# Sinkhorn normalisation with rows on the partitions, column sums on the matrix engine, in a fused attention and feed-forward kernel

## The chip, the cores and the metric

The kernel runs on one core of a Trainium2 chip. A core has a matrix engine (TensorE, PE in the profile; PEld is its weight load), a vector engine (VectorE, DVE), a scalar engine (ScalarE, ACT), GpSimdE (POOL) and SyncE (SP), which only starts transfers here. They work side by side and wait for each other on semaphores. Sixteen DMA engines move data between HBM and the core's memory. Matrix products land in PSUM, which has eight banks (p0 to p7 in this kernel).

The metric is the device time of one execution in microseconds (us); lower is better. The time before is a median of 3 runs. One execution was also profiled; its span runs from its first to its last instruction.

## The reference

Four batches of eight heads each have 768 tokens of 64 features, cut into eight blocks of 96. A small matrix per head, 8x8, is normalised five times by rows and columns (Sinkhorn). With it the blocks of K and V are mixed; then each block of Q attends to the mixed block at its place, and a gated feed-forward layer follows.

```python
P = sort_net                                   # [4, 8, 8, 8]
for _ in range(5):
    P = P - np.max(P, axis=-1, keepdims=True)
    P = np.exp(P)
    P = P / (np.sum(P, axis=-1, keepdims=True) + 1e-09)
    P = P / (np.sum(P, axis=-2, keepdims=True) + 1e-09)
k_sorted = np.einsum('bhij,bhjcd->bhicd', P, k_b).reshape(B, H, S, D)
v_sorted = np.einsum('bhij,bhjcd->bhicd', P, v_b).reshape(B, H, S, D)
...
scores = scale * np.matmul(q_b, k_sb.transpose(0, 1, 2, 4, 3))
attn = softmax(scores)
x = np.matmul(attn, v_sb)                      # to [3072, 512]
...
g = x @ w_gate
out = (g * sigmoid(g) * (x @ w_val)) @ w_out
```

## The kernel before

Work goes in eight units of 384 tokens, two per batch. For each unit the kernel forms scores, softmax, attention output (`xt`) and then the feed-forward products: `g` and `u` (line 520, 12 chunks of 128 features), and the down product (line 548). All matrix work is BF16. The order of all steps is written out by hand in the string `ORDER`; a loop at the end of the kernel calls the step of each word with its arguments, and every engine runs its instructions strictly in that order. A word names the step, its indices, the engine that copies the result out of PSUM (`a` ACT, `d` DVE) and the PSUM bank.

Ahead of `ORDER` stands the opening, which the change is about:

- Loads. SP loads the 32 small matrices (`p_sb`, one per partition, 64 values). POOL issues all large loads, in this order: first half of q of batch 0, K and V of batch 0, weights, the other half of q, and so on. POOL also makes the identity `ident` between the issues.
- Sinkhorn, lines 322 to 338. All 32 matrices lie on 32 partitions, with 64 values each. ACT takes the exponential (331); DVE makes the row sums (332), their reciprocals (333) and products (334), the column sums through a transposed view (335), reciprocals (336) and products (337). The maximum is subtracted once, ahead of the first exponential. Five iterations follow each other, each step dependent on the one before.
- Fills. `busy` (line 245) runs matrix products on constants that nobody reads, so that PE is not idle: 64 of 112 columns at first, and 8 of 112, 10 of 512 and 4 more during the last iterations. `ORDER` has more of them at waits in the first unit.
- `q0_piece` (lines 249 to 259) turns the first q heads, 12 transposes on PE and one ACT copy each, in the fourth and the fifth iteration.
- `make_zk` and `make_bdk` (372 to 388) bring the result to the place where the block mix wants it: `selk` copies each matrix's row of 64 values to the partitions (h, j, ch) of its head on PE, DVE multiplies with a mask and sums (`zk`, `zkr`), and a product with another mask gives `bdk`, a block-diagonal 128x128 matrix per batch. Batch 0 is made on DVE before `ORDER`; the step `late` makes the other three, on POOL.
- Block mix. `k_piece` and `v0_piece` call `mix` (line 283), 16 products per piece of `bdk` with the raw K or V. `ORDER` begins with `late`, five K pieces (`kp`), three V pieces (`v0f`), the sixth K piece, and the scores of the first unit (`tqk`, line 404). K and V are mixed only after their load has landed and `bdk` is there.

Of the kernel before, what the change touches and what calls it, by code (L numbers as in the profile page):

```python
# [9 lines left out]
FP32 = mybir.dt.float32  # L10
BF16 = mybir.dt.bfloat16
# [10 lines left out]
tmt,0,0,a v0f,1,d,p2 v0f,0,a,p3 tst,0,0 texp,0,0 ldv,2 texp,0,2 ldwo,0 v0f,4,d,p6 busy,3,p2 v0t,0,0,d,p7  # L22
v0t,1,0,d,p2 v0t,0,1,a,p3 tav,0,0,p0,p1 tdiv,0,0 v0t,1,1,a,p6 tav,0,1,p4,p5 tdiv,0,1 busy,2,p2 txt,0,0,d,p7
tav,0,2,p2,p3 tdiv,0,2 tav,0,3,p0,p1 txt,0,1,d,p6 q0p,1,0,a,p4 q0p,1,1,a,p5 txt,0,2,a,p7 g,0,2,p2,0,2 g,0,1,p3,0,2
tdiv,0,3 txt,0,3,a,p6 tqk,1,0,p0,p1 tmax,1,0 tqk,1,1,p4,p5 tmax,1,1 vp,1,5,a,p7 g,0,2,p2,2,3 g,0,1,p3,2,3
u,0,1,p6,0,2 ldwo,1 g,0,2,p2,3,4 th,0,2 gs,0,2 g,0,0,p7,0,2 u,0,1,p6,2,3 ldq,3 tmt,1,0,a g,0,1,p3,3,4 th,0,1
u,0,1,p6,3,4 tmt,1,1,d gs,0,1 g,0,0,p7,2,3 tst,1,0 texp,1,0 tst,1,1 texp,1,1 g,0,0,p7,3,4 th,0,0 gs,0,0 us,0,1
hp,0,1 u,0,0,p2,0,2 ldk,2 u,0,2,p3,0,2 u,0,0,p2,2,3 vp,1,3,a,p0 u,0,2,p3,2,3 vp,1,4,d,p1 u,0,2,p3,3,4 h,0,2
u,0,0,p2,3,4 vp,1,2,d,p4 us,0,0 hp,0,0 g,0,3,p5 th,0,3 gs,0,3 u,0,3,p6 h,0,3 kp,1,0,a,p7 kp,1,1,a,p0 g,0,4,p2
th,0,4 gs,0,4 u,0,4,p1 us,0,4 hp,0,4 tqk,1,3,p3,p4 tmax,1,3 tqk,1,2,p5,p6 tmax,1,2 kp,1,2,d,p7 kp,1,3,a,p0  # L30
kp,1,5,a,p2 g,0,5,p1 th,0,5 gs,0,5 u,0,5,p0 us,0,5 hp,0,5 tmt,1,2,a tmt,1,3,d g,0,6,p2 th,0,6 gs,0,6 u,0,6,p7 h,0,6
tst,1,3 texp,1,3 tst,1,2 texp,1,2 tav,1,0,p0,p1 tdiv,1,0 g,0,7,p2 th,0,7 gs,0,7 u,0,7,p7 us,0,7 hp,0,7 txt,1,0,d,p3
tav,1,1,p4,p5 tdiv,1,1 g,0,8,p6 th,0,8 gs,0,8 u,0,8,p0 us,0,8 hp,0,8 tav,1,2,p1,p2 tdiv,1,2 g,0,9,p7 th,0,9 gs,0,9
u,0,9,p3 us,0,9 hp,0,9 txt,1,1,a,p4 vp,1,1,a,p5 txt,1,2,a,p6 g,0,10,p0 th,0,10 gs,0,10 u,0,10,p1 us,0,10 hp,0,10
vp,1,0,a,p2 vtrip,1 ldk,3 g,1,0,p7,0,3 tav,1,3,p3,p4 tdiv,1,3 g,0,11,p5 th,0,11 gs,0,11 u,0,11,p6 us,0,11 hp,0,11
u,1,0,p1,0,3 txt,1,3,d,p0 kp,1,4,d,p2 qp,1,2,d,p3 qp,1,1,d,p4 qp,1,0,d,p5 g,1,0,p7,3,4 th,1,0 gs,1,0 u,1,0,p1,3,4
us,1,0 hp,1,0 g,1,1,p6 th,1,1 gs,1,1 u,1,1,p0 us,1,1 hp,1,1 qk,2,1,p2,p3 rmax,2,1 shift,2,1 expo,2,1 qk,2,2,p4,p5
rmax,2,2 shift,2,2 qp,1,3,a,p1 rsum,2,1 norm,2,1 expo,2,2 rsum,2,2 g,1,2,p7 th,1,2 gs,1,2 u,1,2,p6 us,1,2 hp,1,2
dn,0,2,0,3,p0 dn,0,1,0,4,p2 dn,0,2,3,6 g,1,3,p3 th,1,3 gs,1,3 u,1,3,p1 h,1,3 dn,0,1,4,8 norm,2,2 g,1,4,p4 th,1,4
gs,1,4 dn,0,2,6,9 u,1,4,p5 us,1,4 hp,1,4 ldv,3 g,1,5,p6 th,1,5 gs,1,5 u,1,5,p7 us,1,5 hp,1,5 qk,2,0,p3,p4 rmax,2,0  # L40
# [69 lines left out]
def kernel(  # L110
# [34 lines left out]
    C0 = UT // 128  # L145

# [71 lines left out]
    p_sb = const.tile([BH, NB + 1, NB], FP32, name="p_sb")  # L218
    nc.sync.dma_start(out=p_sb[:, 0:NB, :], in_=sort_net.rearrange("b h i j -> (b h) i j"))
    load_q0(0)  # L220
    load_k(0)
# [5 lines left out]

    fill = const.tile([128, 512], BF16, name="fill")
# [13 lines left out]
    def busy(n, b, cols=512):  # L242

        for _ in range(n):
            nc.tensor.matmul(ps(b, [cols]), lhsT=fill[:, 0:128], rhs=fill[:, 0:cols], start=True, stop=True)  # L245
# [76 lines left out]
    nc.vector.memset(p_sb[:, NB:NB + 1, :], 1e-9)  # L322
    P = p_sb[:, 0:NB, :]
    pbf = const.tile([BH, NB, NB], BF16, name="pbf")
    rowred = const.tile([BH, NB, 1], FP32, name="rowred")
    colred = const.tile([BH, 1, NB], FP32, name="colred")
    nc.vector.reduce_max(rowred[:, :, 0], P, axis=AX.X)
    nc.vector.tensor_tensor(P, P, rowred.to_broadcast([BH, NB, NB]), op=ALU.subtract)
    busy(64, "p7", 112)
    for it in range(N_ITER):  # L330
        nc.scalar.activation(P, P, AF.Exp)
        nc.vector.reduce_sum(rowred[:, :, 0], P, axis=AX.X)
        nc.vector.reciprocal(rowred, rowred)
        nc.vector.tensor_mul(P, P, rowred.to_broadcast([BH, NB, NB]))
        nc.vector.reduce_sum(colred[:, 0, :], p_sb.transpose([0, 2, 1]), axis=AX.X)
        nc.vector.reciprocal(colred, colred)
        nc.vector.tensor_mul(pbf if it == N_ITER - 1 else P, P,
                             colred.to_broadcast([BH, NB, NB]))
        if it == N_ITER - 2:
            q0_piece(0, 0, "a", "p0")  # L340
        if it == N_ITER - 1:
            q0_piece(0, 1, "a", "p1")
            busy(8, "p7", 112)
            busy(10, "p7")
            for _ in range(4):
                nc.tensor.matmul(ps("p7", [UT]), lhsT=fill[:, 0:128], rhs=tr["q", 0][:, HP - 1].rearrange("p i c -> p (i c)"),
                                 start=True, stop=True)
# [42 lines left out]
    def late(b):  # L390
        make_zk(1, B, b)
        for n in range(1, B):
            make_bdk(n, nc.gpsimd)
# [222 lines left out]
```

## Time and profile before

| what | value |
|---|---|
| median of 3 runs | 265.04 us (264.96 to 265.06) |
| the profiled execution, its own time | 265.16 us |
| its span | 263.1 us |
| PE busy | 254.7 us, 97% |
| DVE, ACT, POOL busy | 190.3, 154.2, 116.8 us |
| SP: landing of the small matrices, first DVE step on them | 2.34 us |
| `bdk` of batch 0 done on DVE | 12.75 us |
| first product of the K mix | 13.00 us |
| first product of the V mix | 15.08 us |
| first scores | 17.14 us |

The times in the lower half are counted from the start of the span. In a line of the timeline stand start, length, engine, line of the kernel, operation, what is written and read with its shape, how many instructions are merged, and in brackets how long the engine was idle before and what ended that idle time. A matmul's shape is given as the outputs and columns, such as `128x512`. In the DMA views, packets are counted by size; a share of "16 engines" is the part of all engines' time that the packets of a queue took.

### The profile page before, as it was taken

To read this page: it belongs to the slowest core of one execution; us is meant where nothing else is said; L and a number is where in the kernel's file an instruction comes from. 1 tells how busy PE (TensorE), PEld (TensorE's weight loads), DVE (VectorE), ACT (ScalarE), POOL (GpSimd) and SP (SyncE) were. 2 spreads that over 40 slices of the span, in tenths; PEclk is the share of its full clock that TensorE was granted. 3 is DMA by queue.
4 is the path that set the end of the run, shared out by engine and by line. 5 is a ranking of instruction groups with operands and counts; after the bars stand their busy time and mean duration, and the time that the engine had idled before them with its cause. 6 is when DMAs were issued, how large, how long until landed. Compare 5 with 4: busy or idle time off the path is not lost.

```text
span 263.1 us, 6835 instructions
## 1 busy us (share of the span) xinstructions
PE 254.7 (97%) x2766; PEld 157.1 (60%) x2766; DVE 190.3 (72%) x345; ACT 154.2 (59%) x299; POOL 116.8 (44%) x152
## 2 busy tenths in 40 slices
PE   7878999999999999999999999999999999999995
PEld 7456766665566555665566555665566555655553
DVE  5775877689688896779798776977897778632460
ACT  3246787755467467866476767586566665544422
POOL 8732342433856437135632475226544672431220
PEclk9999999999999999999999999999999999999999
DMA  6999999999980902100294005920110021002103
GB/s 82 215 199 209 216 203 211 204 238 248 157 195 0 161 2 82 44 0 2 120 118 123 2 0 199 118 49 1 52 70 0 2 80 42 0 1 83 40 0 120
DMA packets 33695, 25.60 MB, mean 97 GB/s; under 512 B 21376, under 2 KB 29312, under 8 KB 33664
## 3 DMA queue, kind: packets, MB, share of 16 engines
q0 software_dynamic: 11104, 14.16, 31.4%
q1 hardware_dynamic: 22560, 11.02, 18.2%
q8 instruction: 21, 0.34, 0.5%
q14 instruction: 10, 0.08, 0.1%
HBM read 30.68 MB, written 8.65 MB: 149 GB/s over the span
## 4 chain that ended last, share of the span: by engine, by line
PE 88%; DMA 5%; DVE 3%; issue 1%; ACT 1%; POOL 1%; DVEq 0%; POOLq 0%
PE ps_ps L520 47%; PE ps_ps L548 23%; DMA vn<-in_v_dram 5%; PE ps_ps L497 3%; PE ps_ps L404 3%; PE ps_ps L283 3%; PE ps_ps L508 2%; PE ps_ps L309 2%; PE ps_ps L433 1%; PE ps_ps L270 1%; PE ps_ps L560 1%; DVE qt L240 1%; DVE xn L455 1%; PE ps_ps L447 1%; DVE v L240 0%
## 5 line engine op out<-in xcount | busy, mean ns | idle before, releaser
L539 POOL TENSOR_TENSOR h<-u_sb,gs 128x384 bf16<-128x384 f32 x65 | 58.6, 911 | 64.9 <-DVE gs L533 36.3
L520 PE MATMUL ps_ps<-xt,wg_sb 128*128 128x384 bf16 x384 | 79.8, 327 | 0.0
L520 PE MATMUL ps_ps<-xt,wv_sb 128*128 128x384 bf16 x384 | 79.6, 326 | 0.0
L533 DVE SCALAR_TENSOR_TENSOR gs<-th,ps_ps 128x384 bf16<-128x384 bf16 x96 | 51.4, 543 | 32.4 <-ACT th L525 32.0
L548 PE MATMUL ps_ps<-wo_sb,h 128*128 128x512 bf16 x276 | 70.5, 380 | 0.0
L525 ACT ACTIVATE th<-ps_ps 128x384 bf16<-128x384 f32 x96 | 46.9, 490 | 34.2 <-PE ps_ps L520 32.1
L490 POOL TENSOR_TENSOR en<-e,rs 96x384 bf16<-96x384 f32 x48 | 38.5, 822 | 55.6 <-DVE rs L485 31.1
L520 PEld LDWEIGHTS <-wv_sb 128*128 128x128 bf16 x384 | 37.2, 98 | 24.8
L520 PEld LDWEIGHTS <-wg_sb 128*128 128x128 bf16 x384 | 35.5, 98 | 25.9
L548 PEld LDWEIGHTS <-h 128*128 128x128 bf16 x276 | 26.3, 98 | 25.3 <-issue 0.2
L529 ACT ACTIVATE u_sb<-ps_ps 128x384 f32<-128x384 f32 x65 | 31.8, 490 | 10.9 <-PE ps_ps L520 7.6
L480 ACT ACTIVATE e<-e 96x768 f32<-96x768 f32 x24 | 20.2, 841 | 23.8 <-DVE e L477 23.8
L484 DVE TENSOR_REDUCE rs<-e 96x8 f32<-96x768 f32 x24 | 22.6, 941 | 10.3 <-ACT e L480 10.3
L473 DVE TENSOR_REDUCE rm<-ps_ps 96x8 f32<-96x768 f32 x24 | 22.8, 949 | 4.8 <-PE ps_ps L404 4.3
L477 DVE TENSOR_TENSOR e<-ps_ps,rm 96x768 f32<-96x768 f32 x24 | 22.9, 953 | 0.8
L541 DVE SCALAR_TENSOR_TENSOR h<-ps_ps,gs 128x384 bf16<-128x384 f32 x31 | 17.2, 557 | 2.7
L238 ACT COPY o_sb<-ps_ps 128x512 f32<-128x512 f32 x16 | 9.2, 580 | 8.6 <-PE ps_ps L548 8.6
L497 PEld LDWEIGHTS <-en 96*96 96x96 bf16 x192 | 12.0, 125 | 3.2
L245 PE MATMUL ps_ps<-fill 128*128 128x112 bf16 (+1 forms) x96 | 11.7, 290 | 2.2 <-DVE p_sb L322 1.5
L497 PE MATMUL ps_ps<-ident,en 96*96 96x96 bf16 x192 | 12.5, 209 | 0.0
L238 ACT COPY et<-ps_ps 96x768 bf16<-96x768 bf16 x13 | 10.3, 791 | 3.2 <-PE ps_ps L497 3.1
L238 ACT CAST kt<-ps_ps 128x512 bf16<-128x512 f32 x14 | 7.8, 593 | 3.8 <-PE ps_ps L283 3.7
(97 smaller groups left out, 240.6 us busy)
## 6 DMA issues: line engine op xcount, KB each, us to landing
out_dram<-o_sb SPq DMA_DIRECT2D x23, 256.0 KB, 2.0
kn<-in_k_dram POOLq DMA_DIRECT2D x4, 768.0 KB, 18.6
vn<-in_v_dram POOLq DMA_DIRECT2D x4, 768.0 KB, 14.4
qn<-in_q_dram POOLq DMA_DIRECT2D x3, 768.0 KB, 23.6
vscr<-vm SPq DMA_DIRECT2D x3, 768.0 KB, 3.3
vt<-vscr SPq DMA_DIRECT2D x3, 768.0 KB, 7.9
wg_sb<-in_moe_w_gate_dram POOLq DMA_DIRECT2D x3, 512.0 KB, 18.7
wv_sb<-in_moe_w_val_dram POOLq DMA_DIRECT2D x3, 512.0 KB, 20.4
```

The lines of the kernel that those rows point to most:

```text
L238: nc.scalar.copy(dst, src)
L473: nc.vector.reduce_max(m[:, :, :, 0], st["s", u, hp], axis=AX.X)
L477: nc.vector.tensor_tensor(e, st["s", u, hp], st["m", u, hp].to_broadcast([BLK, 2, HB, BLK]), op=ALU.subtract)
L484: nc.vector.reduce_sum(rs[:, :, :, 0], st["e", u, hp], axis=AX.X)
L490: nc.gpsimd.tensor_tensor(en[:, x], st["e", u, hp][:, x], st["rs", u, hp][:, x].to_broadcast([BLK, HB, BLK]), op=ALU.mult)
L497: nc.tensor.transpose(p[:, x * HB + i, :], st["en", u, hp][:, x, i, :], ident[0:BLK, 0:BLK])
L520: nc.tensor.matmul(st[kind, u, m], lhsT=w[:, kc, ts(m, 128)], rhs=xt[u][:, kc, :], start=(kc == 0), stop=(kc == HP - 1))
L525: nc.scalar.activation(st["th", u, m], st["g", u, m], AF.Tanh, scale=0.5)
L529: nc.scalar.activation(st["us", u, m], st["u", u, m], AF.Copy, scale=0.5)
L533: nc.vector.scalar_tensor_tensor(gs, st["th", u, m], 1.0, st["g", u, m], op0=ALU.add, op1=ALU.mult)
L539: nc.gpsimd.tensor_tensor(h_t[u][:, m, :], st["us", u, m], st["gs", u, m], op=ALU.mult)
L548: nc.tensor.matmul(st["o", u, t], lhsT=h_t[u][:, m, ts(t, 128)], rhs=wo_sb[:, m, :], start=(m == 0), stop=(m == NFC - 1))
```

## The change

The Sinkhorn part is written anew, with what it needs before and after:

- The 256 rows of the 32 matrices lie on the 128 partitions, in two groups `g` of two batches each, with 8 values per row. SP loads them so.
- `exp` on ACT gives the row sums in the same step (`accum_out`), the first one with the maximum as bias. DVE takes the reciprocal and multiplies (`R`, with 1e-9/8 added for the column sum's epsilon).
- The column sums are an FP32 matrix product on PE: `same` is a 128x128 matrix of ones where two rows belong to one head, made from `blk`, which POOL fills with a memset and two selects between the loads of q and K. DVE takes the reciprocal straight from PSUM and multiplies `E`, the row reciprocal and the column reciprocal in one step. The two groups take turns step by step.
- In the last iteration the values are spread by a mask over the heads (`XE`, `X`), and `spread`, one product with `rowi`, puts them where the block mix wants them. `bdk` of batch 0 is made by DVE straight from PSUM; `late` copies the rest once (`z`) and makes three products on POOL as before. `selk`, `mjk`, `pbf`, `zk` and `zkr` are gone.
- A one-element exponential (`warm`) stands at the start of ACT's work.
- The fills are other ones: 48 of 64 columns that write a quarter of the outputs each in turn, 27 of 80 columns, 2 and 13 of 80 in the first iteration, three of 512 in each of the next three, none after. Two groups of fills are gone from `ORDER` (three after `v0f,4`, two after `tdiv,0,1`), and four before the K mix.
- Both q pieces are in the last iteration.

```diff
-    p_sb = const.tile([BH, NB + 1, NB], FP32, name="p_sb")
-    nc.sync.dma_start(out=p_sb[:, 0:NB, :], in_=sort_net.rearrange("b h i j -> (b h) i j"))
+    P = const.tile([128, G, NB], FP32, name="p_sb")
+    nc.sync.dma_start(out=P, in_=sort_net.rearrange("(g b) h i j -> (b h i) g j", b=2))
     load_q0(0)
+    blk = const.tile([128, 2 * H], FP32, name="blk")
+    nc.gpsimd.memset(blk, 1.0)
+    nc.gpsimd.affine_select(out=blk, in_=blk, pattern=[[-NB, 2 * H]], base=0, channel_multiplier=1,
+                            compare_op=ALU.is_ge, fill=0.0)
+    nc.gpsimd.affine_select(out=blk, in_=blk, pattern=[[NB, 2 * H]], base=NB - 1, channel_multiplier=-1,
+                            compare_op=ALU.is_ge, fill=0.0)
     load_k(0)
     load_v(0)
...
+    warm = const.tile([128, 1], FP32, name="warm")
+    nc.vector.memset(warm, 0.0)
+    nc.scalar.activation(warm, warm, AF.Exp)
...
+        for i in range(n):
+            if quarters:
+                r = ts(i % 4, 32)
+                nc.tensor.matmul(ps(b, [cols])[r], lhsT=fill[:, 0:32], rhs=fill[:, 0:cols], start=True, stop=True)
+                continue
             nc.tensor.matmul(ps(b, [cols]), lhsT=fill[:, 0:128], rhs=fill[:, 0:cols], start=True, stop=True)
...
-    nc.vector.reduce_max(rowred[:, :, 0], P, axis=AX.X)
-    nc.vector.tensor_tensor(P, P, rowred.to_broadcast([BH, NB, NB]), op=ALU.subtract)
-    busy(64, "p7", 112)
+    nc.vector.tensor_reduce(nmax, P, axis=AX.X, op=ALU.max, negate=True)
+    same = const.tile([128, 2 * H, NB], FP32, name="same")
+    nc.vector.tensor_copy(same, blk.unsqueeze(2).to_broadcast([128, 2 * H, NB]))
...
+    fills = [((2, "p7", 80), (13, "p7", 80)),
+             ((0, "p7", 80), (3, "p7", 512)),
+             ((0, "p7", 80), (3, "p7", 512)),
+             ((0, "p7", 80), (3, "p7", 512))]
+    busy(48, "p7", 64, True)
+    busy(27, "p7", 80)
     for it in range(N_ITER):
-        nc.scalar.activation(P, P, AF.Exp)
-        nc.vector.reduce_sum(rowred[:, :, 0], P, axis=AX.X)
-        nc.vector.reciprocal(rowred, rowred)
-        nc.vector.tensor_mul(P, P, rowred.to_broadcast([BH, NB, NB]))
-        nc.vector.reduce_sum(colred[:, 0, :], p_sb.transpose([0, 2, 1]), axis=AX.X)
-        nc.vector.reciprocal(colred, colred)
-        nc.vector.tensor_mul(pbf if it == N_ITER - 1 else P, P,
-                             colred.to_broadcast([BH, NB, NB]))
...
-            busy(8, "p7", 112)
-            busy(10, "p7")
...
+        last = it == N_ITER - 1
+        for g in range(G):
+            nc.scalar.activation(E[g], P[:, g, :], AF.Exp, bias=nmax[:, g:g + 1] if it == 0 else 0.0,
+                                 accum_out=rs[g])
+        for g in range(G):
+            nc.vector.reciprocal(rs[g], rs[g])
+            nc.vector.tensor_scalar(R[g] if last else R[g][:, :, 0], wide(E[g]) if last else E[g], rs[g], 1e-9 / NB,
+                                    op0=ALU.mult, op1=ALU.add)
+        if last:
             q0_piece(0, 0, "a", "p0")
+        for g in range(G):
+            nc.tensor.matmul(colsum[g][:, 0:NB * CH if last else NB], lhsT=same.rearrange("p c i -> p (c i)"),
+                             rhs=R[g].rearrange("p j ch -> p (j ch)") if last else R[g][:, :, 0], start=True, stop=True)
+            if not last:
+                busy(*fills[it][g])
+            elif g == 1:
+                q0_piece(0, 1, "a", "p1")
+        for g in range(G):
+            if last:
+                nc.vector.tensor_tensor(XE[g].rearrange("p h (j ch) -> p h j ch", ch=CH),
+                                        mask8.unsqueeze(2).unsqueeze(3).to_broadcast([128, H, NB, CH]),
+                                        E[g].unsqueeze(1).unsqueeze(3).to_broadcast([128, H, NB, CH]), op=ALU.mult)
+                nc.vector.reciprocal(cs[g], colsum[g])
+                nc.vector.scalar_tensor_tensor(X[g], XE[g], rs[g], cs[g].unsqueeze(1).to_broadcast([128, H, NB * CH]),
+                                               op0=ALU.mult, op1=ALU.mult)
+            else:
+                nc.vector.reciprocal(cs[g][:, 0:NB], colsum[g][:, 0:NB])
+                nc.vector.scalar_tensor_tensor(P[:, g, :], E[g], rs[g], cs[g][:, 0:NB], op0=ALU.mult, op1=ALU.mult)
...
-            nc.gpsimd.tensor_copy(selk, ident[0:BH, 0:BH].unsqueeze(2).to_broadcast([BH, BH, 16]))
+            mask8 = const.tile([128, H], FP32, name="mask8")
+            nc.vector.tensor_tensor(mask8, blk[:, 0:H], blk[:, H:2 * H], op=ALU.add)
...
-    def make_zk(b0, b1, b):
...
+    def spread(out, g):
+        nc.tensor.matmul(out.rearrange("p b i -> p (b i)"), lhsT=X[g].rearrange("p h c -> p (h c)"),
+                         rhs=rowi.rearrange("p b i -> p (b i)"), start=True, stop=True)
...
+    def late(bk):
+        p = ps(bk, [B, NB])
+        for g in range(G):
+            spread(p[:, ts(g, G), :], g)
+        z = const.tile([128, B - 1, NB], FP32, name="z")
+        nc.vector.tensor_copy(z, p[:, 1:B, :])
         for n in range(1, B):
-            make_bdk(n, nc.gpsimd)
+            make_bdk(n, nc.gpsimd, z[:, n - 1, :])
...
-    make_zk(0, 1, "p2")
-    make_bdk(0, nc.vector)
-    busy(4, "p7")
+    z0 = ps("p2", [G, NB])
+    spread(z0, 0)
+    make_bdk(0, nc.vector, z0[:, 0, :])
+    busy(0, "p7")
```

## The prediction

> **What bounds the kernel now.** I read the page first, then the waits of TensorE (PE) by stretches, then the chain that ended last up to 18 us, then the timeline of the first 18 us, and last the DMA view in narrow windows. On the page PE is busy for 254.7 of 263.1 us, so most of the span cannot be moved by this change. The waits of PE from 30 us on are one line:
>
> ```profile
> PE ps_ps L404 <- DVE qt L240: 0.3, 1, 0.3
> ```
>
> After 30 us PE runs one fixed order with 0.3 us of waiting. Whatever the start gains or loses goes through to the end one to one, and all that the change touches lies before. The chain in order of time says what sets the start (start, length, what):
>
> ```profile
> 2.86 12.18 DMA vn<-in_v_dram
> 15.04 0.04 issue
> 15.08 0.97 PE ps_ps L283 x48
> 16.05 1.09 ACT vT L238 x2
> ```
>
> The block mix of V waits until V has landed at 15.04. The Sinkhorn chain is not in it. The timeline shows how near it comes; one iteration, then its end:
>
> ```profile
> 6.37 0.26 ACT L331 ACTIVATE p_sb<-p_sb 32x64 f32<-32x64 f32 x1 [1.52 <-DVE p_sb L337]
> 6.66 0.21 DVE L332 TENSOR_REDUCE rowred<-p_sb 32x8 f32<-32x64 f32 x1
> 6.90 0.19 DVE L333 RECIPROCAL rowred<-rowred 32x8 f32<-32x8 f32 x1
> 7.13 0.21 DVE L334 TENSOR_TENSOR p_sb<-p_sb,rowred 32x64 f32<-32x64 f32 x1
> ...
> 7.91 0.21 DVE L337 TENSOR_TENSOR p_sb<-p_sb,colred 32x64 f32<-32x64 f32 x1
> ...
> 8.15 0.26 ACT L331 ACTIVATE p_sb<-p_sb 32x64 f32<-32x64 f32 x1 [1.52 <-DVE p_sb L337]
> ...
> 12.46 0.29 DVE L384 TENSOR_TENSOR bdk<-m,zkr 128x128 bf16<-128x128 f32 x1
> ...
> 13.00 1.46 PE L283 MATMUL ps_ps<-bdk,kn 128*64 128x64 bf16 x80
> ...
> 15.08 0.95 PE L283 MATMUL ps_ps<-bdk,vn 128*64 128x64 bf16 x48 [0.63 <-DMA vn<-in_v_dram]
> 15.86 0.42 PE L283 MATMUL ps_ps<-bdk,kn 128*64 128x64 bf16 x16
> ```
>
> An iteration takes 1.78 us (6.37 to 8.15). Dependent steps start 0.23 to 0.29 us apart, however small. The five K pieces run from 13.00 to 14.46, then PE waits 0.63 us for V. So the K pieces may start as late as 15.08 - 1.46 = 13.62 without moving anything; an earlier start gains nothing while V lands at 15.04.
>
> **The change part by part.**
>
> Loads. SP's first load brings 256 rows of 32 bytes in place of 32 rows of 256; it landed at 2.3. The nearest row for small pieces is the first q load: 942 packets below 512 B (the DMA window below) in some 2.4 us, 59 per engine, so 41 ns each; with 16 pieces per engine instead of 2 it lands 0 to 0.6 us later, and I take 0.3. POOL's queue gets a memset and two selects between the q load and the K load. Rows: a 128x1 memset 0.10, the select that makes ident 0.29, so K, V and all behind them are issued about 0.7 us later, until the removed selk copy (0.64) gives it back at the second V load. Cover: the queue moves data in order, and K's large packets follow q's small ones:
>
> ```profile
> DMA packets 1016, 0.81 MB, mean 203 GB/s; under 512 B 942, under 2 KB 942, under 8 KB 1016
> ```
>
> That is 4 to 8 us: q's small packets first, and the 74 large ones from 5.9 on, where the rate of the slices jumps. q's issue ran from 1.24 to 2.31 and its first packets went at 3.2, 0.9 us later; K, issued at 3.0 for 0.57 us, is ready by 4.5, while q still moves. So 0. Without that cover it would be 0.7.
>
> First column sum. From the landing at 2.6: maximum 0.25, exponential with its row sum 0.5, reciprocal 0.23, product to PE 0.27: 3.9. In front of it PE has 48 fills of 64 columns on a quarter of the outputs and 27 of 80. The clock of the present fills is told by their pace (stretch, then PE's busy time and count in it):
>
> ```profile
> 1.50:4.90 3.40, 3.40 (x38) 3.40 (x39) 1.00 0.54 48
> 5.30:6.30 1.00, 1.00 (x24) 0.97 (x20) 1.00 1.69 232
> ```
>
> 89 ns for 112 columns at first, 42 ns later. 27 fills of 80 columns at the slow pace are 27 x 64 ns = 1.7 us. Of the quarter fills there is no row: at most 51 ns (one after the other), at least 18 ns, the pace of the K mix, which streams as many columns to half the outputs at the fast clock (1.46 us / 80). That mix slowed by 89/42 is 38; quarters leave room for twice as many side by side, 19, and I take the middle, 28. The fills then end at 1.46 + 1.3 + 1.7 = 4.5 (bounds 4.0 and 5.6), and the first column sum runs at 4.5.
>
> One iteration, one group: exponential to VectorE (DVE) 0.29, the row sum's read-out, reciprocal 0.23, product to PE 0.27, PE to DVE 0.22, reciprocal 0.25, product to ACT 0.25: 1.51 without the unknowns. The read-out costs 0 if the exponential carries it, and 0.29 if it is a second ACT instruction as long as the first; I take 0.2, nearer to an instruction of its own. The FP32 product costs 0 or a second pass, 0.18 by the row of selk (load 0.09, matmul 0.18, half hidden); I take 0.1. Sum 1.81, bounds 1.51 and 1.98. The second group adds four short DVE steps and two on ACT per iteration; they fit into the waits of the first, since a step occupies its engine for less than its 0.2 us of latency (independent steps at 6.13 and 6.27 start 0.14 apart). Its exponential stands behind the first's read-out; if they don't fit, that is the upper bound. So the present 1.78 becomes 1.81: seven dependent steps for seven.
>
> The end. From the last column sum: 0.32 to DVE, reciprocal 0.25, then X0, the masked E1, a reciprocal, X1 and bdk in DVE's order, four at 0.29 and one at 0.19 less some overlap: 1.85 in all (1.6 to 2.1). XE0 lies in the first wait. The spread of group 0 lies beside X1. The q pieces now sit here on PE (12 transposes, 0.4 us each) and their two copies on ACT (0.77 each), behind the last exponentials; the second holds bank p1, which the first K piece needs; it is done about 0.3 us before.
>
> Sum: 4.5 + 4 x 1.81 + 1.85 = 13.6, where the K pieces start, against 13.00 now and 13.62 allowed: 0.0 us, with the cover used up. Bounds: 4.0 + 6.0 + 1.6 = 11.6 and 5.6 + 7.9 + 2.1 = 15.6.
>
> What then follows in the queue: z is one copy of 0.2 where zk and zkr took 0.36 + 0.35 on DVE; the three K evictions (1.88) end near 16.1, before the sixth K piece needs DVE at 16.40. POOL's three bdk products still wait for older loads until 18.68. The removed fills (three at 23.83, two at 27.39) lie in waits for DVE: the first ends at 24.65 and the next transposes wait for an eviction until 24.70. 0 to -0.1. Their cover lost, PE idles 0.9 us there.
>
> So the profiled execution stays at 265.16 (span 263.1, 2.0 around it), 0.12 above the median of 265.04. I predict 265.1 as median: 265.04 and less than 0.1 for the spent cover.
>
> **The rivals.**
>
> *Slower: the Sinkhorn becomes the bound.* From 13.62 on each us counts. With quarter fills at 51 ns (first column sum at 5.6) and the sum's other values it starts K at 14.7: +1.1, 266.1. For it: the sum has no slack left, and one cost at its high end is enough. Against: the same costs may lie lower, and 1.5 us an iteration would give back 1.2 us.
>
> *Slower: a cold PE.* The present fills keep PE nearly without a gap from 1.46 to 10.3. The new ones leave some 0.6 us idle in each 1.8 us iteration (three fills of 0.21 and two column sums), and about 1 us more at the end. If PE is at the slow pace when K starts, it will stay so about as long as the present fills took from their start to the change of pace, 1.46 to 5.1: 3.7 us, in which 3.7 x 42/89 = 1.7 us of work is done: +2.0 with K at 13.6, 267.0. [...]
>
> *Faster: V lands earlier.* In the DMA view of 8 to 12 us one line stands out:
>
> ```profile
> q8 instruction: 1, 0.02, 1.5%
> ```
>
> One instruction packet took 1.5% of 16 engines for 4 us, 0.96 us on one engine. From 13.6 to 15.05 all but two of 282 packets are the small ones of the next weights: V's last two came alone, on an engine about 1 us behind the others. PE's program changes, so this fetch can move. If it falls after 14.0, V is there at 14.1; the K pieces must also be done, which needs a start by 12.6 (read-out and second pass free): -1.0, 264.1. Against: in program order 126 matmuls and ten FP32 products stand ahead of K where 118 stood, so PE asks for its next instructions no later than now, and a fetch that comes earlier takes the same 0.96 us out of the same queue.
>
> **How the numbers follow.** Forecast (264.7 to 265.5) 0.53; Sinkhorn late by over 0.5 us 0.23, at 266.1; cold PE 0.07, at 267.0; V earlier 0.17, at 264.1. 0.2% is 0.53 us, about what a measurement of this kernel can tell from no change: faster 0.17, same 0.53, slower 0.30. The range from 264.1 to 266.4 leaves out the cold PE and the tails of the other two, near 0.2.
>
> **What would show it.** K's first matmul at 13.2 to 14.0, and the V mix at 15.1 directly behind the fifth K piece: right. Iterations 1.8 us apart: the step costs are right; 1.5, read-out and second pass are free. If the V mix starts with a wait for V over 0.6 us, the Sinkhorn got shorter for nothing. It is wrong if the V mix starts before 14.6 or after 15.6, if the K mix runs at over 30 ns a matmul, or if PE waits after 30 us by more than 0.5 us.

## The result, and the profile after

The changed kernel takes 269.22 us (268.96 to 270.81), the kernel before 265.01: a ratio of 1.0168, 95% interval 1.0143 to 1.0193. It is slower by 4.2 us, and slower than the whole predicted range. The profiled execution took 269.41 us, span 267.5 against 263.1.

PE's waits from 30 us on, in the profile of after (who waits, for whom, total us, times, longest):

```profile
PE ps_ps L446 <- DVE qt L253: 0.3, 1, 0.3
PE ps_ps L502 <- DVE xn L497: 0.3, 1, 0.3
```

So nothing was lost behind 30 us: the first scores start at 21.69 instead of 17.14 (+4.55), and the span is 4.3 longer. The loss lies at the start. The chain of waits in order of time (start, length, what):

```profile
16.43 0.81 ACT q0t L251
17.24 0.04 issue
17.28 1.93 PE ps_ps L300 x33
19.21 0.02 issue
19.24 1.30 DVE kt L253 x2
20.54 0.04 issue
20.57 1.09 ACT vT L251 x2
```

In before this chain held V's landing at 15.04. Now V has long landed (at 15.77) when the V mix starts at 19.39; the Sinkhorn, and then the K mix, set everything. One undisturbed iteration and the end, in the timeline of after (start, length, engine, line, operation):

```profile
10.62 0.21 ACT L365 ACTIVATE E<-p_sb 128x8 f32<-128x8 f32 x1 [2.13 <-DVE p_sb L391]
...
10.74 0.19 ACT L365 ACTIVATION_READ_ACCUMULATOR E<-p_sb 128x1 f32 x1
...
11.26 0.23 DVE L370 TENSOR_SCALAR R<-E,rs 128x8 f32<-128x8 f32 x1
...
11.54 1.02 PE L375 MATMUL ps_ps<-R,same 128*128 128x8 f32 x4
...
12.18 0.21 DVE L390 RECIPROCAL cs<-ps_ps 128x8 f32<-128x8 f32 x1 [0.36 <-PE ps_ps L375]
...
12.42 1.44 PE L262 MATMUL ps_ps<-fill 128*128 128x512 bf16 x3
...
12.74 0.21 ACT L365 ACTIVATE E<-p_sb 128x8 f32<-128x8 f32 x1 [1.39 <-DVE p_sb L391]
...
13.70 0.23 DVE L370 TENSOR_SCALAR R<-E,rs 128x16 f32<-128x16 f32 x1
13.79 0.61 PEld L274 LDWEIGHTS <-qh 128*64 128x64 bf16 x12 [0.83 <-issue]
13.79 0.85 PE L274 MATMUL ps_ps<-ident,qh 128*64 128x128 bf16 x12
...
14.57 1.04 PE L375 MATMUL ps_ps<-R,same 128*128 128x16 f32 x4
...
17.28 2.35 PE L300 MATMUL ps_ps<-bdk,kn 128*64 128x64 bf16 x80 [0.41 <-ACT q0t L251]
```

Three things are to be seen. The period is 2.12 us, and PE to DVE takes 0.64 of it (11.54 to 12.18). The last column sum runs at 14.57, though its first group was ready at about 13.5: three fills and 12 transposes stood ahead of it in PE's queue. And PE's own pace tells its clock: the five K pieces, unchanged work, take 2.35 us where they took 1.46, and a fill of 512 columns 0.48 (three in 1.44) where it took 0.26 in before (four in 1.04):

```profile
11.84 1.04 PE L245 MATMUL ps_ps<-fill 128*128 128x512 bf16 x4
```

PE is at half clock: in dense below, three such fills take the same 1.44 (from 10.60) at a recorded clock of 0.50. The trace also holds records of the clock. They begin with the clock's first change, and the clock column of the stretches counts a stretch without a record as 1.00, so a start at half clock can be seen by the pace alone. The first record of after is the change to full clock at 19.97 us, that of before at 5.01, where the pace of its fills changes too.

There are records for the profiled execution alone. Its mean granted clock is 1.000; the other five executions of after have 0.967 to 0.981 and about the same times. In all3 below a mean of 0.981 goes with 10.24 us at half clock after a first rise, in dense 0.967 with 17.07. By that estimate the clock came up earlier in the other five and was lost again for 10 to 17 us.

The third period of the Sinkhorn is longer still, 3.17 us, with this in it:

```profile
8.48 0.89 DVE L370 TENSOR_SCALAR R<-E,rs 128x8 f32<-128x8 f32 x1
8.62 0.75 DVE L368 RECIPROCAL rs<-rs 128x1 f32<-128x1 f32 x1
8.71 0.63 POOL L404 MEMSET rmb<- 96x128 bf16 x4
```

The same small DVE instruction takes 0.23 elsewhere.

### The profile page after: what moved, and what is told of

It reads as the page before. It is cut to its first block, busy times and chain, and to the rows that moved or that the text cites. A ratio compares the mean times of both kernels' runs of the same rounds, so it can differ in the third digit from the quotient of the medians.

```text
span 267.5 us, 6891 instructions
## 1 busy us (share of the span) xinstructions
PE 256.1 (96%) x2758; PEld 160.6 (60%) x2789; DVE 192.3 (72%) x355; ACT 156.5 (59%) x315; POOL 116.8 (44%) x154
## 4 chain that ended last, share of the span: by engine, by line
PE 91%; DVE 5%; issue 2%; ACT 1%; DVEq 0%
PE ps_ps L562 47%; PE ps_ps L590 22%; PE ps_ps L539 3%; PE ps_ps L446 3%; PE ps_ps L300 3%; PE ps_ps L262 2%; PE ps_ps L550 2%; PE ps_ps L375 1%; PE ps_ps L326 1%; PE ps_ps L475 1%; PE ps_ps L287 1%; PE ps_ps L602 1%; DVE qt L253 1%; DVE kt L253 1%; DVE xn L497 1%
## 5 line engine op out<-in xcount | busy, mean ns | idle before, releaser
L590 PE MATMUL ps_ps<-wo_sb,h 128*128 128x512 bf16 x249 | 66.5, 380 | 1.1
L251 ACT CAST xt<-ps_ps 128x384 bf16<-128x384 f32 x17 | 7.5, 483 | 4.1 <-PE ps_ps L550 3.9
L262 PE MATMUL ps_ps<-fill 128*128 128x80 bf16 (+1 forms) x54 | 8.8, 327 | 1.0 <-ACT ett L482 0.7
```

The lines of the kernel that those rows point to most:

```text
L251: nc.scalar.copy(dst, src)
L590: nc.tensor.matmul(st["o", u, t], lhsT=h_t[u][:, m, ts(t, 128)], rhs=wo_sb[:, m, :], start=(m == 0), stop=(m == NFC - 1))
```

## The experiments

All milestones are from the timeline of each run's profiled execution, in us; the time is the median of all its executions, and before took 264.85 to 265.19 beside them. The two are not always the same execution: the profiled one took 271.54 in dense, 268.39 in old_nofill, 268.33 in warm_all and 271.47 in best. The last column says when the clock was full, by the trace's clock records up to 31 us; warm's trace has none, and there the pace says it. Unless a line says otherwise, a run is the changed kernel with the edit shown.

| run | first column sum | last column sum | K mix | V mix | scores | time | full clock |
|---|---|---|---|---|---|---|---|
| before | | | 13.00 | 15.08 | 17.14 | 265.01 | from 5.01 |
| after | 4.10 | 14.57 | 17.28 | 19.39 | 21.69 | 269.22 | from 19.97 |
| dense | 6.00 | 14.87 | 17.58 | 19.68 | 22.48 | 270.11 | 5.97 to 9.39, from 26.45 |
| pool | 4.10 | 13.93 | 16.65 | 18.76 | 21.44 | 269.20 | from 20.30 |
| queue | 4.09 | 13.57 | 16.28 | 18.39 | 21.18 | 268.93 | from 20.73 |
| all3 | 6.02 | 14.24 | 16.96 | 19.07 | 21.48 | 269.84 | 6.30 to 9.72, from 19.96 |
| iterfill | 4.10 | 14.90 | 17.08 | 18.34 | 20.40 | 268.52 | from 14.33 |
| old_nofill | | | 14.49 | 16.34 | 18.39 | 267.23 | 15.91 to 22.74, from 26.15 |
| warm | 4.95 | 13.31 | 15.49 | 16.75 | 19.08 | 266.93 | no record |
| warm_pool | 5.45 | 13.37 | 15.55 | 16.82 | 19.36 | 266.97 | from 6.01 |
| warm_all | 4.80 | 15.06 | 17.24 | 18.50 | 20.56 | 268.04 | from 14.17 |
| warm_tt | 5.45 | 12.78 | 14.96 | 16.22 | 18.85 | 266.45 | from 5.82 |
| warm_end | 5.31 | 13.33 | 15.31 | 17.74 | 20.21 | 267.90 | 5.14 to 15.38, from 18.79 |
| warm_bf16 | 5.22 | 12.73 | 14.89 | 16.16 | 19.21 | 267.01 | from 4.96 |
| warm_fetch | 4.88 | 12.29 | 14.47 | 15.79 | 17.84 | 265.94 | from 4.23 |
| best | 3.95 | 11.29 | 13.27 | 15.72 | 20.72 | 269.98 | 6.33 to 13.15, 16.57 to 19.98, from 30.22 |
| best2 | 3.96 | 11.18 | 13.15 | 14.77 | 16.83 | 264.77 | from 5.54 |

The stretches at full and at half clock between two changes last 3.41, 6.83, 10.24 or 17.07 us, one, two, three or five times 3.41.

**dense: whole fills at the start.**

```diff
-    busy(48, "p7", 64, True)
-    busy(27, "p7", 80)
+    busy(48, "p7", 112)
```

> After, with the first fills put back to whole 128-column products of 112 columns (48 of them, in place of 48 quarter fills and 27 of 80). Theory cold PE: the clock comes up near 5.3 us as before and stays up; the first column sum is 1.1 us later (5.2 for 4.1), each FP32 column-sum pair shrinks from 0.64 to about 0.35 us ahead of DVE (4 times -0.3), the three 512 fills and the first 12 q transposes ahead of the last column sum take half (-1.0), the K mix takes 1.5 for 2.35 us (-0.9): first scores near 19.5 for 21.7, time 267.0 (266.4 to 267.6). Theory that the step costs (DVE, ACT, FP32) are what is long and the clock is only a bystander: 1.1 us later start and nothing back, 270.3.

Measured 270.11, near the second theory's number, but for another reason. Stretches of the profile of dense (stretch, its length, busy time of each engine with counts, granted clock, DMA):

```profile
6.00:7.00 1.00, 1.00 (x22) 0.98 (x19) 0.55 (x3) 0.05 (x1) 1.00 (x2) 1.00 1.05 201
7.00:8.00 1.00, 0.34 (x6) 0.23 (x2) 0.93 (x6) 0.55 (x4) 0.89 (x4) 1.00 1.02 203
8.00:9.00 1.00, 0.93 (x6) 0.50 (x6) 0.84 (x6) 0.24 (x2) 1.00 (x4) 1.00 1.00 197
9.00:10.00 1.00, 0.48 (x3) 0.28 (x2) 0.93 (x6) 0.36 (x3) 1.00 (x5) 0.69 1.09 221
10.00:12.00 2.00, 2.00 (x8) 1.01 (x8) 1.50 (x9) 0.60 (x4) 1.45 (x2) 0.50 1.01 209
24.00:26.00 2.00, 1.78 (x16) 0.95 (x17) 1.86 (x3) 0.24 (x1) 0.16 (x1) 0.50 1.08 189
26.00:28.00 2.00, 1.28 (x23) 0.81 (x19) 0.95 (x1) 0.94 (x2) 0.55 (x1) 0.89 1.23 206
```

The clock came up at 5.97 us, after 4.4 us of whole fills, was lost at 9.39, in the thin stretch of column sums and three fills per iteration, and did not return before 26.45. While it was up, one iteration took 1.81 us (exponentials at 6.95 and 8.76), the value that I had predicted; after it was lost, 2.12 again. In that stretch, from 6.0 to 9.4, PE was busy for some 2.5 of 3.4 us, and its longest wait was 0.66. And at 10 to 12 it is shown busy for 2.00 of 2.00 us at a clock of 0.50; in after it is shown busy without a gap from 10.30 to 16.30, and the clock came up at 19.97. Being shown as busy is not enough to raise it.

**pool, queue, all3: POOL's work away, the last fills away, all three.**

```diff
-            nc.gpsimd.tensor_scalar(selm, ..., -1.0, None, op0=ALU.mult)
-            for t in rmb:
-                nc.gpsimd.memset(t, 0.0)
+        if it == 2:
+            nc.scalar.mul(selm, sel.unsqueeze(2).to_broadcast([128, HB, BLK]), -1.0)
+        if it in (1, 2):
+            for t in rmb[2 * it - 2:2 * it]:
+                nc.vector.memset(t, 0.0)
```

```diff
-             ((0, "p7", 80), (3, "p7", 512))]
+             ((0, "p7", 80), (0, "p7", 512))]
```

> After, with selm made by ACT (one instruction in the third iteration) and the four rmb memsets on DVE, so that POOL computes nothing beside the third iteration. Theory that POOL's instructions stall DVE there: the third period goes from 3.17 to 2.2 us and the time falls by 0.8 to 1.0 us, to 268.3. Rival, that DVE's 0.55 and 0.89 us instructions there have another cause: no change, 269.2.

> After, without the last three 512-column fills (fourth iteration). Theory that PE's own queue holds the last column sum back: it runs at 13.6 instead of 14.6, the copy of the second q piece frees bank p1 a microsecond earlier, K starts at 16.2 for 17.3, time 268.1 to 268.3. Rival: the fills keep the clock, and taking them away makes what follows slower or moves nothing: 269.2 or more.

> The three edits together (dense first fills, POOL's work moved, last 512 fills gone). If the three causes are separate they nearly add up: first column sum 5.2, four periods of 1.8, K mix from 14.6 to 15.2 at 18 ns a product, and then V's landing near 15.7 is the bound: scores near 17.8, time 265.3 to 266.2. If the cold clock alone is the cause, no better than the dense run, 267.0.

The two mechanisms are there, the gains are not. In pool the third period falls from 3.17 to 2.45, K starts 0.63 earlier, and the scores come only 0.25 earlier. In queue the last column sum moves to 13.57 and K to 16.28, as expected, and the scores come 0.5 earlier. What comes earlier is done by a PE that is still cold (the clock came up at 20.30 in pool and 20.73 in queue, for 19.97), so the time hardly moves. all3 lost the clock at 9.72, like dense.

**iterfill: the first fills as they were, those of the iterations denser.**

```diff
-    fills = [((2, "p7", 80), (13, "p7", 80)),
-             ((0, "p7", 80), (3, "p7", 512)),
-             ((0, "p7", 80), (3, "p7", 512)),
+    fills = [((2, "p7", 80), (20, "p7", 80)),
+             ((0, "p7", 80), (5, "p7", 512)),
+             ((0, "p7", 80), (5, "p7", 512)),
```

> After, with its own first fills (48 quarters, 27 of 80) and only the fills of the iterations made denser, as in warm (20 of 80 for 13; five of 512 for three, twice). If the first fills' thinness alone keeps the clock down, PE fills the iterations at half clock and the clock comes up once a stretch of them is dense enough, late; the longer fills then stand ahead of the column sums: 269 to 271. If the iterations are what matters, the clock comes up by 9 us and stays: 266.5 to 267.5.

268.52 (267.87 to 270.44), a little better than expected of the first case: the clock came up at 14.33, so the K mix ran at 18 ns a product, but the long cold fills held the column sums. Neither the first fills nor those of the iterations alone do it.

**old_nofill: the kernel before, without its first fills.**

```diff
-    busy(64, "p7", 112)
...
-            busy(8, "p7", 112)
-            busy(10, "p7")
```

> Before, without its first 64 fills and without the 8 and 10 fills of the last iteration (the four before K stay): the old Sinkhorn untouched, PE cold. Theory cold PE: K still starts at 13.0, its five pieces take 2.35 for 1.46 us, the V mix starts near 15.4, and PE runs at half clock until some 3.4 to 7 us after K's start; scores near 18.5 to 19, time 266.5 to 268. If a cold start costs little here (the wait for V covers it): 265.0 to 265.5.

267.23, ratio 1.0095 (1.0071 to 1.0118): the old Sinkhorn with a cold PE loses 2.2 us. Its timeline shows where; the four fills ahead of K and the K mix itself are longer:

```profile
12.41 1.89 PE L245 MATMUL ps_ps<-fill 128*128 128x512 bf16 x4
14.22 0.34 PE L373 MATMUL ps_ps<-pbf,selk 32*128 32x64 bf16 x3
14.49 2.02 PE L283 MATMUL ps_ps<-bdk,kn 128*64 128x64 bf16 x80
```

In before those fills took 1.04 and K's pieces 1.46. K did not start at 13.0 as expected: the fills ahead of it held it. The clock came up at 15.91, within the K mix, and in this execution, which took 268.39, it was lost once more, from 22.74 to 26.15 us. The other three have a granted clock of 0.998 to 1.000 and took 266.91 to 267.25, so the loss of 2.2 stands without that.

**warm: dense at the start and in the iterations.**

```diff
-    busy(48, "p7", 64, True)
-    busy(27, "p7", 80)
+    busy(42, "p7", 112)
```

The `fills` are those of iterfill.

> After, with the first fills as 42 of 112 columns on the whole array (as in the run dense, six fewer), 20 of 80 behind the first column sums for 13, and five of 512 for three in the second and third iteration. In the run dense the granted clock came up and was lost again at 9.3 us, with column sums and three fills per iteration. Theory that PE's work is too thin in the iterations: with PE filled nearly without a gap the clock stays at 1.00 from 5.5 us to the end, periods are 1.8 (the one beside POOL's selm up to 2.2), the last 512 fills and q transposes take half, K starts at 14.3 to 15.3 and V's landing near 15.7 sets the rest: scores near 17.9, time 265.6 to 266.6. Rival, that FP32 column sums bring the clock down whatever stands beside them: the clock falls again near 9 us, 269 to 270.

266.93 (266.81 to 267.07), ratio 1.0077 (1.006 to 1.0094). By the pace the clock stays at full, and 2.3 of the 4.2 us are back:

```profile
15.49 1.46 PE L300 MATMUL ps_ps<-bdk,kn 128*64 128x64 bf16 x80
```

That is the main cause shown, by adding and by taking away. The forecast was 0.3 too low: K starts at 15.49, and DVE still loses time. In the timeline of warm, three products and what POOL did beside them:

```profile
6.16 0.90 POOL L200 DMA_DIRECT2D qh<-in_q_dram  x1
...
8.71 0.63 POOL L403 MEMSET rmb<- 96x128 bf16 x4
...
10.68 0.77 POOL L209 DMA_DIRECT2D wv_sb<-in_moe_w_val_dram  x1
```

```profile
6.43 0.63 DVE L369 TENSOR_SCALAR R<-E,rs 128x8 f32<-128x8 f32 x1
...
8.87 0.50 DVE L369 TENSOR_SCALAR R<-E,rs 128x8 f32<-128x8 f32 x1
...
11.00 0.45 DVE L369 TENSOR_SCALAR R<-E,rs 128x8 f32<-128x8 f32 x1
```

The ends coincide: 6.43 + 0.63 and 6.16 + 0.90 are both 7.06, 11.00 + 0.45 and 10.68 + 0.77 both 11.45, and 9.37 lies just behind the memsets' 9.34. A mere DMA issue on POOL does it too.

**warm_pool, warm_all: where POOL's work and loads stand.** warm_pool is warm with the edit of pool; warm_all besides:

```diff
+    load_k(0)
+    load_v(0)
     blk = const.tile([128, 2 * H], FP32, name="blk")
...
-    load_k(0)
-    load_v(0)
...
-    busy(42, "p7", 112)
+    busy(34, "p7", 112)
```

> The run warm, with selm on ACT and the rmb memsets on DVE. If POOL's instructions stall DVE also with a fast PE, K starts 0.3 to 1.0 us earlier than in warm; the time falls only if K, not V's landing, is the bound: 265.6 to 266.2. If they don't, K starts no earlier.

> The run warm_pool, with the making of blk behind K's and V's issue (they go out 0.7 us earlier) and 34 first fills for 42, so that the first column sum runs at 4.6. If the issue order is what makes V land at 15.7 instead of 15.0, V lands at 15.0 to 15.1; K starts at 13.6 to 14.3; scores 17.1 to 17.6 and time 264.9 to 265.6, level with before. If V's landing does not depend on the issue order, it stays at 15.7 and the time is that of warm_pool.

warm_pool: 266.97, no gain; the moved work only lets POOL's DMA issues run earlier, and they meet DVE instead (products of 0.36 and 0.34). warm_all: 268.04 with one execution at 266.94; with eight fills fewer the clock came up at 14.17 in the profiled one. V landed at 14.12 here, but at 14.57 in warm with the later issue and at 15.52 in warm_pool with the same later issue. The landing of V moved between 14.0 and 15.9 over all runs, so that the worth of the issue order stays unsettled.

**warm_tt: another form of the same DVE instruction.**

```diff
-            nc.vector.tensor_scalar(R[g] ..., E[g], rs[g], 1e-9 / NB, op0=ALU.mult, op1=ALU.add)
+            nc.vector.tensor_tensor(R[g] ..., E[g], rs[g].to_broadcast([128, NB]), op=ALU.mult)
```

> The run warm, with the product of E and the row reciprocal (R) made by tensor_tensor with a broadcast second input instead of tensor_scalar; the 1e-9/8 that tensor_scalar adds is left out. In warm four of the tensor_scalars took 0.37 to 0.63 us for 0.23, each ending with a POOL instruction or DMA issue that was under way. Theory that it is the form of DVE's instruction that waits for POOL: the products take 0.21 to 0.27 as in before, periods fall from 2.28, 2.23 and 2.08 to 1.8 to 1.9, K starts 0.8 to 1.2 earlier (14.3 to 14.7), time 265.9 to 266.2. Rival, that any DVE instruction waits there: no change, 266.9.

All ten products take 0.17 to 0.18, the periods are 1.74, 1.89 and 1.80, and from the first to the last column sum it takes 7.33 us where warm took 8.36. So it is the form of this instruction that waits for POOL. DVE's three-input product still waited once: at 7.63 in warm_fetch below it took 0.48 beside POOL's `selm`, for 0.23 elsewhere. The time falls only to 266.45 (1.0045, 1.0031 to 1.006), above the expected 266.2, and the waits of PE say why:

```profile
PE ps_ps L300 <- issue: 0.4, 1, 0.4
```

PE stops inside the V mix for nothing that the profile shows.

**warm_end, warm_bf16: the end, and the price of FP32.** warm_end: q pieces ahead of the column sums of the last two iterations, both `XE` before the first `cs`, `X1` behind `bdk`, `late` behind two K pieces, and three fills of 512 for five in the third iteration. The second edit is warm_bf16's.

```diff
-        if last:
-            q0_piece(0, 0, "a", "p0")
+        if it >= N_ITER - 2:
+            n = it - N_ITER + 2
+            q0_piece(0, n, "a", f"p{n}")
...
+    finish(0)
...
     make_bdk(0, nc.vector, z0[:, 0, :])
+    finish(1)
```

```diff
-    same = const.tile([128, 2 * H, NB], FP32, name="same")
+    same = const.tile([128, 2 * H, NB], BF16, name="same")
-    R = [const.tile([128, NB, CH], FP32, name=f"R{g}") for g in range(G)]
+    R = [const.tile([128, NB, CH], BF16, name=f"R{g}") for g in range(G)]
```

`finish(g)` is the reciprocal `cs` and the product `X` of group g.

> The run warm, with the q pieces ahead of the column sums of the fourth and the fifth iteration (as in before), both masked products ahead of the first column reciprocal, X1 behind bdk, late behind two K pieces, and three 512 fills for five in the third iteration. In warm it takes 2.18 us from the last column sum (13.31) to K (15.49), with the second q copy and bdk ending together. Theory that DVE's order and the q copy make the end long: 1.6 to 1.8, K 0.4 to 0.6 earlier, 266.3 to 266.6. Rival, that something else (the copies of the K pieces behind it) takes it back: 266.9.

> The run warm, with R and the matrix of ones in BF16: each column sum is one load and one product instead of two and two. Theory: the price of FP32 at full clock is about 0.1 to 0.15 us per column sum on the path (I had put 0.1 into the sum): K starts 0.5 to 0.7 earlier, 266.3 to 266.5. If the second pass is hidden: 266.9.

warm_end is inconclusive: 267.90 with one execution at 266.78; in the profiled one the end took 1.98 for 2.18, but the clock was lost from 15.38 to 18.79, and `late` stood in the way of the K mix. Whether the two fills fewer or the new order lost it was not taken apart. warm_bf16: an iteration with hardly a wait for POOL takes 1.65 (exponentials at 10.21 and 11.86) against 1.81 in dense, so FP32 costs some 0.16 per iteration at full clock, and K starts 0.6 earlier than in warm. The time doesn't fall (267.01): PE stops for 0.8 us in its V mix.

**best: all of them, first column sum at 4.0.** The edits of warm_tt, warm_end and warm_bf16, and:

```diff
-    busy(42, "p7", 112)
+    busy(26, "p7", 112)
...
-    fills = [((2, "p7", 80), (20, "p7", 80)),
+    fills = [((4, "p7", 112), (20, "p7", 112)),
```

> The three together, and 26 first fills with four of 112 between the first two column sums and 20 behind them, so that the first column sum runs at 4.0 and PE stays filled. If the causes add: K starts at 12.3 to 13.3, before V has landed (14.0 to 15.8 in the runs so far), and V is the bound again: 264.2 to 265.7. If the first column sums are thin enough to cost a window of clock: 266 to 268.

269.98 (267.39 to 271.47), with K at 13.27. The timeline of the profiled execution, which took 271.47:

```profile
15.72 1.24 PE L300 MATMUL ps_ps<-bdk,vn 128*64 128x64 bf16 x45
19.36 0.25 PE L300 MATMUL ps_ps<-bdk,vn 128*64 128x64 bf16 x3 [2.41 <-issue]
```

PE stands for 2.41 us in the middle of one row of equal products. Counted from its start, with an FP32 product as two, this is behind product 223, and so are the stops of warm_tt and warm_bf16. In the DMA records one 16 KB instruction packet passed from 17.04 to 17.97 here, 14.69 to 15.58 in warm_tt and 15.14 to 16.08 in warm_bf16, and PE went on 1.4 to 1.5 us after each ended. In before it passed from 11.34 and in after from 8.71, early enough. The expectation below has these times 0.24 us late, and so the restart too near. The clock was lost twice as well.

**warm_fetch: as much PE time, more instructions early.** The edit to warm_tt:

```diff
-             ((0, "p7", 80), (5, "p7", 512)),
+             ((0, "p7", 80), (24, "p7", 112)),
```

> The run warm_tt, with 24 fills of 112 columns for the five of 512 in the second iteration: as much PE time, 19 products more. In warm, warm_tt, warm_bf16 and best PE stopped in the V mix for up to 2.4 us without a wait that the profile shows, always behind its 223rd product, and went on 1.1 to 1.3 us after an instruction packet had passed the DMA engines (at 14.9 to 17.3 us); in before and after that packet passed at 11.6 and 8.9 us. Theory that the packet is asked for when PE has come through about its 95th product: it passes 2 to 4 us earlier (11 to 13 us), V mix without a stop, scores near 18.3, time 0.3 to 0.5 below warm_tt, 266.0. Rival, that the stop has another cause: it stays, 266.4.

265.94, ratio 1.0036 (1.0023 to 1.005). The packet passes from 11.17. In the DMA view of warm_tt it is found in the stretch from 14 to 16 us, in that of warm_fetch from 10 to 13:

```profile
q8 instruction: 1, 0.02, 2.8%
q8 instruction: 1, 0.02, 2.0%
```

The V mix runs through:

```profile
14.47 1.46 PE L300 MATMUL ps_ps<-bdk,kn 128*64 128x64 bf16 x80
15.79 0.95 PE L300 MATMUL ps_ps<-bdk,vn 128*64 128x64 bf16 x48
16.57 0.42 PE L300 MATMUL ps_ps<-bdk,kn 128*64 128x64 bf16 x16
17.84 0.74 PE L446 MATMUL ps_ps<-kt,q0t 64*96 64x96 bf16 x24 [0.86 <-ACT vT L251]
```

From K's start to the scores it is 3.37 us, 3.89 in warm_tt. The time alone would not decide it, since the two runs' ratios overlap in their intervals. But the packet moved 3.5 us forward with nothing but the fills changed, and the stop is gone: both halves of the theory came out as forecast, that the stop is PE waiting for instructions, and that short fills early make it ask sooner. No view shows the wait itself.

**best2: everything, and PE filled to the K mix.** The edit to best:

```diff
+    fills = [((4, "p7", 112), (22, "p7", 112)),
+             ((0, "p7", 80), (28, "p7", 112)),
+             ((0, "p7", 80), (4, "p7", 512)),
+             ((0, "p7", 80), (4, "p7", 512))]
...
+    busy(2, "p7")
     z0 = ps("p2", [G, NB])
     spread(z0, 0)
...
+    busy(2, "p7")
```

> The run best, with more and shorter fills early (22 of 112 behind the first column sums, 28 of 112 in the second iteration), four of 512 in the third and fourth iteration, and two of 512 on either side of the first spread, so that PE is filled to the K mix and passes its 95th product by 9 us. If the clock and the instruction packet are what best lost by: the clock stays up, no stop in the V mix, K starts at 13.0 to 13.6, scores at 17.0 to 17.8, time 264.9 to 265.7. If the gaps that are left still cost a window of clock: 266 to 268.

264.77 (264.59 to 265.41) beside 265.00; the ratio over all runs is 0.9998 (0.9989 to 1.0007). The new Sinkhorn, with the costs found taken out, is level with the old one. Its timeline:

```profile
13.15 0.69 PE L300 MATMUL ps_ps<-bdk,kn 128*64 128x64 bf16 x32
...
14.77 0.95 PE L300 MATMUL ps_ps<-bdk,vn 128*64 128x64 bf16 x48
15.55 0.42 PE L300 MATMUL ps_ps<-bdk,kn 128*64 128x64 bf16 x16
16.83 0.74 PE L448 MATMUL ps_ps<-kt,q0t 64*96 64x96 bf16 x24 [0.86 <-ACT vT L251]
```

V landed at 14.73, just ahead of its mix. The scores are 0.31 earlier than in before. A start still earlier would meet V's landing, as in before. best2 also has what the changed kernel had not, BF16 column sums and another order at the end, so it bounds the sum of the costs and does not price each.

## Why the prediction was wrong

The frame held: after 30 us the shift goes through nearly one to one, and the loss is K's lateness and its slower mix. The prediction's 13.62 for the latest harmless start of K adds the whole 1.46 that the K mix is shown busy; but the V mix starts 1.26 us behind K's start where nothing holds it (warm), so the bound is 15.08 - 1.26 = 13.82. The 4.55 of the scores are then 3.46 of lateness (17.28 - 13.82), 0.85 of slower K mix (2.11 us to the start of V for 1.26) and 0.24 behind the start of V (2.30 for 2.06), whose mix begins at half clock too.

- **The step that failed** is the one that the sum never names: behind the first fills, every duration of PE in it was taken at full clock. The rival "a cold PE" got 0.07. I took the idle 0.6 us of each iteration as too short to lose the clock by, which was my estimate and which no run shows. That asked only how the clock is lost. In the profiled execution the new start did not raise it before 19.97 us: 2.7 us of quarter and 80-column fills, then FP32 column sums of eight columns and three fills per iteration. Whether the first fills were too thin or too short was not taken apart; those of dense are wider and last 4.4 us. And dense shows that the clock is lost without a gap longer than 0.66 us: at full it lasted 3.41 us, and the half clock after it 17.07, five times as long. The rival's price of +2.0 was for the K mix with K on time; a cold PE also makes the Sinkhorn itself longer, which I did not put together with the other slower rival. Both came at once. I had looked at the idle gaps alone and passed over the work between them.
- **Loads.** The small matrices were 0.26 later (2.60 for 2.34; I took 0.3). K and V were issued 0.7 later, as worked out. K's mix never waited for K; for V see warm_all.
- **First column sum**, put at 4.5: 4.10. A quarter fill takes 17 ns, not 28, even at the cold pace.
- **One iteration**, put at 1.81: 1.81 at full clock in dense, so the sum was right there; 2.12 with a cold PE, and 2.51 in the first and 3.17 in the third period. Four of them took 10.47 us (4.10 to 14.57) instead of 7.24. The read-out is an instruction of its own, 0.19 (taken 0.2). The FP32 product takes 0.64 to DVE cold and 0.42 in dense at full clock, where I had 0.32; in BF16 it took 0.20.
- **Not in the sum at all:** DVE's wait for POOL. I had taken 0.27 from the product to PE from rows of before, in which the DVE instructions of an iteration take 0.19 to 0.27 each, beside POOL's `selm` too (7.41 to 8.59), and changed its form without asking whether the new one waits for POOL. What makes it wait was not shown. The runs show the ends that coincide in warm (7.06, 11.45), and a product with two inputs that takes 0.17 beside POOL's memsets in warm_tt (9.00). Not every overlap costs: in the middle of POOL's `selm` a `tensor_scalar` at 7.86 in dense took 0.24, and a product with two inputs at 8.51 in warm_fetch 0.17.
- **The end**, put at 1.85: 2.71 in after, 2.18 in warm_fetch. The q pieces were called hidden. At half clock the last fills, with the transposes behind them, held the last column sum by 1.0 (queue), and the second copy held K by 0.41. Another order at full clock takes 1.97 (best2); the 0.1 left over 1.85 was not taken apart.
- **The instruction packet.** That it would come no later than now held: 8.71 for 11.34. That it sets V's landing stays open. In old_nofill, the kernel before with its packet at 19.09, V landed at 14.07 for 15.04, as the rival had it; in dense, too, no packet passed before V's last one, and V landed at 15.90. What mattered was its other side, which I did not consider, and only in the experiments with fewer instructions.
- **The signs I named.** The V mix started at 19.39, far behind the bound of 15.6. PE waited after 30 us for 0.6 in all, 0.3 at most at a time, and the K mix took 29 ns a product, just under the bound of 30 that I had given for a cold PE. The bound was too high: 2.35 us for 1.46 is plain enough.

The ledger of the 4.2 us, each median less that of before beside it: clock 2.3 (after to warm), form of the product 0.7 (warm_tt), PE's stop for instructions 0.3 (warm_fetch), and 0.9 left. The warm runs had brought the stop in by their fewer instructions. By the medians as they stand the middle two are 0.5 and 0.5; between them the split is not sure, since before itself differed by 0.2. In the rest K starts at 14.47 for the 13.6 of the sum: first column sum 0.4 late, iterations 1.85 for 1.81, end 0.3 long.

## What to carry to other kernels

Fill work has to be judged by the clock that it keeps, not by PE's busy share: look at the pace of an unchanged product. In these runs it took a long run of wide products in front (42 of 112 columns in warm) and hardly any thin stretch behind: dense, with 48 in front and three fills per iteration, lost the clock after 3.41 us. When an instruction's form changes, ask which other engine it can wait for, and look for ends that coincide (here a `tensor_scalar` of 0.63 us for 0.23, and a DMA issue on POOL, both ending at 7.06 in warm). Before merging many short PE instructions into few long ones, find the instruction packet in the DMA view and see how far ahead of its use it passes: in best it ended at 17.97, in the middle of PE's stop of 2.41 us; in warm_fetch it passed from 11.17, and the stop was gone.

## What was not expected of the hardware

- A matrix engine that the profile shows as busy at 2.00 of 2.00 us stayed at a clock of 0.50 (dense, 10 to 12 us). Which of the thin products (FP32 sums, transposes, quarter fills) count least was not tried apart.
- Where the clock was lost, the times of the same program spread: after took 268.96 us at a mean clock of 0.981 and 270.81 at 0.967, best 267.39 at 0.979 and 271.47 at 0.974; before, at 0.998 to 1.000, took 264.4 to 265.5. With the same 42 first fills it came up between 4.23 and 6.01 us (warm_fetch, warm_pool); what sets the moment was not shown.
- `tensor_scalar` on eight values per partition took up to 0.89 us beside POOL's memsets (after), and up to 0.63 beside a mere DMA issue on POOL (warm), for 0.23 elsewhere.
- PE stood 2.41 us (best), for its own instructions by the experiment warm_fetch, and in three runs (best, warm_tt, warm_bf16) restarted 1.4 to 1.5 us after the packet had passed.
